# Windowed attention and two feed-forward stages on one core: PSUM shared out in halves of banks during the attention

## The chip, the cores and the metric

The kernel runs on one core of one Trainium2 chip. The metric is the device time of one execution in microseconds (us); the time of a kernel is the median of several runs. The core has a matrix engine (TensorE, PE in the profile, its weight loads PEld), a vector engine (VectorE, DVE), an activation engine (ScalarE, ACT), GpSimd (POOL) and queues for DMA (SP). Matrix products land in PSUM, which has eight banks; one bank holds 512 fp32 numbers for each of 128 partitions. DVE and ACT read the products from there.

## The reference

```python
# q, k, v: (4, 8, 576, 64), causal attention in a window of 64
scores = scale * q @ k.T ;  mask = (rel >= 0) & (rel < 64)
x = softmax(where(mask, scores, -1e9)) @ v        # -> (2304, 512)
# feed-forward 1: d_model 512, d_ff 1536
xn = x / sqrt(mean(x*x) + 1e-6) * rms_g
x = (silu(xn @ w_gate) * (xn @ w_val)) @ w_out
# feed-forward 2: d_model 512, d_ff 2048
out = (relu(x @ w_in) ** 2) @ w_out2
```

## The kernel before

All is kept transposed (features on the partitions). Each matrix product of the feed-forward parts is made of three: both operands are split into a high and a low part, and high times high, low times high and high times low are added up in PSUM (lines L608, L610, L612).

**Attention.** There are 36 blocks of 64 tokens. For a block PE makes the scores (L430), DVE adds the mask (L435), ACT takes the exponential (L437), PE transposes (L443), ACT or DVE copies (`pt`), PE multiplies by v (L453), DVE scales into `acc` (L458), and ACT or DVE sums the squares (L463, L465). Four blocks make a tile of 256 tokens, nine tiles in all. For a tile `rms` makes one small product (L479) and about nine tiny DVE instructions for the normalising factor, and then for each of the four blocks: DVE writes the normalised block into one of two buffers `xw` (L502), PE transposes it in two pieces (L506), ACT or DVE copies the high part from PSUM (L510, recorded by the helper at L238), and DVE subtracts for the low part (L511, recorded at L239).

**Feed-forward 1, first stage.** While the attention of later tiles goes on, the first two of the twelve slices of d_ff are worked on for each tile of 256 tokens: `up` makes for each slice two products of 12 matmuls (gate and value), ACT takes tanh of the gate (L653), two DVE instructions combine them (L654 reads the gate, L655 the value), and ACT and DVE split the result (`ah`, `al`). `down` makes four products of 6 matmuls, and ACT or DVE copies them to `acc`. So the first stage has 9 x 4 products of 12 matmuls and 8 x 4 of 6 ahead of the second stage. The second stage, on tiles of up to 512 tokens, begins at 171 us of the span, and feed-forward 2 comes behind it.

**PSUM.** Each `ps[i]` is one bank. Scores use banks 4 and 5, the transposes of the softmax 6, the products with v 7. The feed-forward products take whole banks 0, 1, 2 in turn (`mm_ring`), though a product of 256 columns fills half of one. `rms` uses bank 3 (`R_BANK`): the small product is in its first half, and the four blocks of a tile take its two halves in turn (`half`).

**Order.** Nothing is issued in the order in which the program is written. `Schedule.add` records a step with the keys that it reads and writes and a cost; `issue` then runs through a model of the engines and emits the steps in the order in which they could start there. Its keys for `rms` are those of the halves, `("ps", 3, 0)` and `("ps", 3, 1)`, and for the products those of whole banks. The semaphores are not set from these keys: the framework below sets them from the emitted order and the memory that instructions touch. Until the first product, PE's idle time in that model is filled with products nobody reads (L1015, into bank 0).

Of the kernel before, what the change touches and what calls it, by code (L numbers as in the profile page):

```python
# [16 lines left out]
ALU = mybir.AluOpType  # L17
# [13 lines left out]
EPS = 1e-6  # L31
# [196 lines left out]
def attn_moe_moe2(ctx: ExitStack, tc: tile.TileContext, qT, kT, vw, w1, w2, w3, w4, rms_g, out):  # L228
# [76 lines left out]
        return [("R", off // G32 + i) for i in g]  # L305

    ps = [psum.tile([P, 512], F32, name=f"ps{i}") for i in range(8)]
    mm_ring = Ring([0, 1, 2])

    fp = first_ctx.enter_context(tc.tile_pool(name="first", bufs=1, side="right"))  # L310
    s_ring = ring(fp, "s", S1, [P, N1])
# [21 lines left out]
    def at(*a, **k):  # L333
        attn_steps.append(sc.add(*a, **k))
# [134 lines left out]
        return ("pe", 0.45, 0.28, scores, [q] + kk, sk, 0.0), ("", softmax), ("pe", 0.46, 0.24, pv, [v, pt], [xk], 0.02), ("", result)  # L469


    half = [0]

    def rms(t, rank, part):
        nb = t[1]
        r = small["r"].next()
        ss = ps[R_BANK][:, :nb]
        m, y, z = (T[r][:, i, :nb] for i in range(3))
        at("pe", 0.3, lambda: nc.tensor.matmul(ss, T["comb"], T[part][:, :nb], start=True, stop=True), r=[(part, i) for i in range(nb)] + ["comb"], w=[("ps", R_BANK, 0)], rank=rank)  # L479
        tiny = lambda fn, rd=(): at("dve", 0.07, fn, r=rd, w=[r])  # L480
        tiny(lambda: nc.vector.tensor_scalar(m, ss, 1.0 / DM, EPS, op0=ALU.mult, op1=ALU.add), [("ps", R_BANK, 0)])


        tiny(lambda: nc.vector.tensor_scalar(y.bitcast(I32), m.bitcast(I32), -0.5, float(0x5F3759DF), op0=ALU.mult, op1=ALU.add))
        tt = lambda o, i, j: tiny(lambda: nc.vector.tensor_tensor(o, i, j, op=ALU.mult))
        stt = lambda o, i, j, v, op: tiny(lambda: nc.vector.scalar_tensor_tensor(o, i, v, j, op0=op, op1=ALU.mult))
        tt(z, m, y)
        tt(z, z, y)
        stt(z, z, z, -10.0 / 3.0, ALU.add)
        stt(y, z, y, 5.0, ALU.add)  # L490
        tt(z, m, y)
        stt(z, z, y, -0.5 * RS * RS, ALU.mult)
        stt(y, z, y, 1.5, ALU.add)
        for i, n in enumerate(blks(t)):
            half[0] ^= 1
            xw = xw_ring.next()
            pk = ("ps", R_BANK, half[0])
            x = T["acc"][:, :, n * WIN : (n + 1) * WIN]
            hi, lo = (xview(c, n * WIN, WIN) for c in ("xh", "xl"))
            x_ps = ps[R_BANK].rearrange("p (e i k) -> p e i k", e=2, i=2)[:, half[0]]  # L500
            kk = lambda c, n=n: allk(c, (n, 1))
            at("dve", c_dve(256), lambda i=i, x=x, xw=xw: nc.vector.scalar_tensor_tensor(T[xw].rearrange("p (a d) -> p a d", a=NP), x, T[r][:, 1, i : i + 1], T["gg"], op0=ALU.mult, op1=ALU.mult), r=[r, "gg"] + kk("acc"), w=[xw], port=True)  # L502

            def turn(xw=xw, x_ps=x_ps):
                for j in range(2):
                    nc.tensor.transpose(x_ps[:, j], T[xw][:, j * P : (j + 1) * P], T["ident"])  # L506

            at("pe", 0.108 * 2 + 0.1, turn, r=[xw, "ident"], w=[pk], rank=rank + 0.01 * (i + 1))
            xt = x_ps.rearrange("p i (h s) -> p (i h) s", h=2)
            at(AD, c_ad(256, True), lambda e, xt=xt, hi=hi: copy(e, hi, xt), r=[pk], w=kk("xh"))  # L510
            at("dve", c_dve(256), lambda xt=xt, hi=hi, lo=lo: sub(lo, xt, hi.bitcast(F32)), r=[pk] + kk("xh"), w=kk("xl"))  # L511
# [509 lines left out]
    def record(k):  # L1021

        stage, fs, t = seq[k]
        ends = [f for f in fs if end_of[stage, f] == k]
        if k < n_first:
            at_until(T1[min(k + 1, n_first - 1)])
            if k == n_first - 1:
                closed.append(sc.add("none", 0.001, close, after=list(attn_steps)))
                free.extend(range(W0, W0 + W1))
        if k == n_first:  # L1030
            flush()
            closed2.append(sc.add("none", 0.001, close2, after=list(first_steps) + closed))
            mm_ring.extend([3, 4])
            EXTRA[:] = 0.09, 0.1, 0.25
            a_ring.slots, a_ring.i = list(range(A1, A1 + A2)), 0
            s_ring.slots, s_ring.i = [f"s{S1 + i}" for i in range(S2)], 0
        if k >= n_first:
            while jobs and len(jobs) > n_jobs * (1 - (k - n_first + 1) / (len(seq) - n_first)):
                fn, *more = jobs.pop(0)
                fn(*more)  # L1040
        prefetch()
        a = {}
        for pos, f in enumerate(fs):
            a[f] = up(stage, f, t)
            if f in ends:
                for m in range(2):
                    free.append(w_slot.pop((stage, f, m)))
                prefetch()
            if pos == min(state.get("hold", 0), len(fs)) - 1:
                flush()  # L1050

        def finish():
            down(stage, fs, a, t, first_of[stage, t[0]] == k)
            for f in ends:
                free.append(w_slot.pop((stage, f, "down")))
            prefetch()


        state["prev"], state["hold"] = finish, min(2, len(a_ring.slots) - len(fs))
# [120 lines left out]
```

## Time and profile before

| | us |
|---|---|
| median of 3 runs | 914.86 (913.35 to 915.72) |
| profiled execution, its own time | 914.39 |
| its span, first to last instruction | 912.7 |
| PE busy | 894.8 (98% of the span) |
| PEld / DVE / ACT busy | 839.3 / 698.0 / 573.1 |

The time of the profiled execution is 1.7 us above its span and 0.5 us below the median. Busy time counts an engine's instructions; that of PE is modelled, since matmuls overlap. The granted TensorE clock is full from the first slice to the last. A row of waits names the instruction that waited, the one that released it, the sum, the count and the longest.

### The profile page before, as it was taken

The page shows a single profiled execution, that of the slowest core. Times are in us where ns is not written, and L with a number is a line of the kernel's source. Part 1 is how long each engine was busy: PE and PEld are TensorE (multiplying, and loading weights), DVE is VectorE, ACT ScalarE, POOL GpSimd, SP SyncE. Part 2 cuts the span into 40 slices and gives each one's busy share as a digit, 9 for nine tenths or more (in the row PEclk, how much of TensorE's full clock was granted, in tenths as well). Part 3 has the DMA queues.
Part 4 walks back from the last instruction along what each step waited for, and adds up shares of the span by engine and source line. Part 5 has one row for each costly group of instructions (what it writes and reads, how often), then busy time and mean ns, then how long its engine had stood idle before and what let it go on. Part 6 is the DMA issues. An engine that isn't in the chain of part 4 may idle for free.

```text
span 912.7 us, 17324 instructions
## 1 busy us (share of the span) xinstructions
PE 894.8 (98%) x6598; PEld 839.3 (92%) x6598; DVE 698.0 (76%) x1663; ACT 573.1 (63%) x1227; POOL 42.7 (5%) x45
## 2 busy tenths in 40 slices
PE   7889999999999999999999999999999999999997
PEld 6778899989988988988988999999999999999997
DVE  5999987677767877777768558667789976777786
ACT  6998875666666667666667556655557655555561
POOL 1000000000000100000000000000002300000011
PEclk9999999999999999999999999999999999999999
DMA  8856520246535735534556136272717373718142
GB/s 248 267 180 216 164 87 2 93 163 240 181 109 179 239 124 179 204 113 169 189 199 231 56 115 211 79 249 75 267 57 270 106 269 107 274 51 288 36 169 98
DMA packets 67203, 149.50 MB, mean 164 GB/s; under 512 B 6704, under 2 KB 25136, under 8 KB 67120
## 3 DMA queue, kind: packets, MB, share of 16 engines
q1 hardware_dynamic: 66592, 148.26, 47.6%
q8 instruction: 52, 0.85, 0.4%
q14 instruction: 31, 0.25, 0.1%
q10 hardware_dynamic: 528, 0.13, 0.1%
HBM read 114.30 MB, written 34.08 MB: 163 GB/s over the span
## 4 chain that ended last, share of the span: by engine, by line
PE 86%; DVE 11%; DMA 1%; ACT 1%; issue 1%
PE ps L884 19%; PE ps L820 18%; PE ps L608 15%; PE ps L610 15%; PE ps L612 15%; DVE sm L435 2%; DVE R L239 1%; DVE Q L239 1%; DVE xw L502 1%; PE ps L453 1%; DVE acc L458 1%; PE ps L430 1%; PE ps L443 1%; PE ps L1015 1%; DMA Q<-w 1%
## 5 line engine op out<-in xcount | busy, mean ns | idle before, releaser
L820 PE MATMUL ps<-R 128*128 128x288 f32 x1344 | 187.5, 296 | 0.8 <-DVE ps L238 0.6
L820 PEld LDWEIGHTS ps<-R 128*128 128x128 f32 x1344 | 181.6, 189 | 1.8 <-DVE ps L238 0.8
L884 PE MATMUL ps<-L,R 128*128 128x288 f32 x630 | 169.7, 297 | 1.5 <-DVE acc L892 1.3
L884 PE MATMUL ps<-Q,L 128*128 128x288 f32 x480 | 133.4, 297 | 0.0
L884 PEld LDWEIGHTS ps<-L,R 128*128 128x128 f32 x630 | 118.6, 188 | 2.5 <-DVE acc L892 2.0
L608 PE MATMUL ps<-R 128*128 128x256 f32 (+3 forms) x444 | 99.8, 347 | 0.6 <-ACT R L238 0.6
L610 PE MATMUL ps<-R 128*128 128x256 f32 (+3 forms) x444 | 97.6, 342 | 0.0
L612 PE MATMUL ps<-R 128*128 128x256 f32 (+3 forms) x444 | 97.3, 341 | 0.0
L238 ACT CAST L<-Q 128x512 fp32r<-128x512 f32 (+3 forms) x104 | 57.3, 565 | 62.7 <-DVE Q L651 56.0
L892 DVE TENSOR_TENSOR acc<-ps,acc 128x288 f32<-128x288 f32 x136 | 61.5, 456 | 41.0 <-PE ps L884 38.5
L884 PEld LDWEIGHTS ps<-Q,L 128*128 128x128 f32 x480 | 90.7, 189 | 0.0
L608 PEld LDWEIGHTS ps<-R 128*128 128x128 f32 x444 | 75.1, 189 | 8.0 <-ACT R L238 0.7
L610 PEld LDWEIGHTS ps<-R 128*128 128x128 f32 x444 | 75.6, 189 | 6.6
L612 PEld LDWEIGHTS ps<-R 128*128 128x128 f32 x444 | 75.6, 189 | 6.6
L238 DVE COPY acc<-ps 128x448 f32<-128x448 f32 (+4 forms) x81 | 47.8, 590 | 38.6 <-PE ps L612 19.4
L651 DVE TENSOR_TENSOR Q<-ps,Q 128x512 f32<-128x512 f32 (+2 forms) x50 | 31.9, 638 | 59.1 <-PE ps L612 57.4
L238 ACT COPY acc<-ps 128x288 f32<-128x288 f32 (+4 forms) x108 | 47.3, 439 | 42.0 <-PE ps L884 27.4
L240 DVE TENSOR_TENSOR L<-Q,L 128x512 fp32r<-128x512 f32 (+2 forms) x94 | 71.0, 761 | 1.9 <-ACT L L238 1.8
L868 ACT CAST L<-Q 128x576 fp32r<-128x576 f32 (+1 forms) x45 | 33.9, 756 | 59.1 <-PE ps L884 59.0
L681 ACT COPY ps<-acc 128x448 f32<-128x448 f32 (+2 forms) x97 | 53.1, 554 | 23.3 <-DVE acc L238 21.4
L239 DVE TENSOR_TENSOR Q<-Q 128x288 f32<-128x288 f32 (+1 forms) x96 | 60.0, 625 | 3.5 <-ACT Q L833 0.4
L437 ACT ACTIVATE sm<-sm,nb 128x128 f32<-128x128 f32 (+1 forms) x144 | 55.4, 388 | 10.4 <-DVE nb L435 10.4
(124 smaller groups left out, 1722.4 us busy)
## 6 DMA issues: line engine op xcount, KB each, us to landing
Q<-w SPq DMA_DIRECT2D x68, 512.0 KB, 4.4
R<-su SPq DMA_DIRECT2D x16, 1024.0 KB, 6.1
su<-L SPq DMA_DIRECT2D x24, 512.0 KB, 3.2
sd<-L SPq DMA_DIRECT2D x24, 512.0 KB, 3.2
R<-su SPq DMA_DIRECT2D x16, 768.0 KB, 5.0
v<-vw SPq DMA_DIRECT2D x36, 256.0 KB, 3.8
R<-sd SPq DMA_DIRECT2D x8, 1024.0 KB, 5.7
L<-sd SPq DMA_DIRECT2D x8, 1024.0 KB, 7.7
```

The lines of the kernel that those rows point to most:

```text
L238: copy = lambda e, out, in_: nc.scalar.copy(out, in_) if e == "act" else nc.vector.tensor_copy(out, in_)
L239: sub = lambda out, a, b: nc.vector.tensor_tensor(out, a, b, op=ALU.subtract)
L240: two = lambda e, out, a, b, op: (nc.vector if e == "dve" else nc.gpsimd).tensor_tensor(out, a, b, op=op)
L437: at("act", 0.39, lambda p=p: nc.scalar.activation(T[sm][:, p, :nk], T[sm][:, p, :nk], AF.Exp, bias=T[nb][:, p : p + 1], scale=-1.0, accum ...
L608: nc.tensor.matmul(acc, wh, xh, start=(i == 0 and not seeded), stop=False, skip_group_check=seeded)
L610: nc.tensor.matmul(acc, wl, xh, start=False, stop=False, skip_group_check=seeded)
L612: nc.tensor.matmul(acc, wh, xl, start=False, stop=(i == n - 1), skip_group_check=seeded)
L681: add("act", c_act(n), lambda b=b, dst=dst: nc.scalar.copy(ps[b][:, :n], dst), r=keys("acc", c, t), w=[("ps", b)])
L820: nc.tensor.matmul(bank, w_, x_, start=(start and i == 0), stop=(i == len(terms) - 1), skip_group_check=True)
L868: sc.add("act", c_act(m * PN), lambda z=z, o=o, m=m: nc.scalar.copy(z("h"), e(o, m)), r=ek(o, m), w=bk("h"))
L884: nc.tensor.matmul(bank, w_, x_, start=(start and i == 0), stop=(i == len(terms) - 1), skip_group_check=True)
L892: sc.add("dve", c_dve(PN), lambda: nc.vector.tensor_tensor(y(i, j), src, y(i, j), op=ALU.add), r=[key], w=yk(i, j))
```

## The change

Banks 0 and 1 are each cut in two halves of 256 columns, and during the first stage the feed-forward products take these four halves in turn: 0 first half, 0 second half, 1 first half, 1 second half. Bank 2 is thereby free and goes to `rms`, whose small product and whose blocks take four halves in turn, of banks 3, 2, 3, 2. With the second stage the products go back to whole banks, as before five of them, in the order 2, 3, 4, 0, 1 (before 3, 4, and then 0 to 2 from where the ring stood). The keys of the schedule are now those of the halves.

```diff
     ps = [psum.tile([P, 512], F32, name=f"ps{i}") for i in range(8)]
-    mm_ring = Ring([0, 1, 2])
+    for b in range(2):
+        ps += [ps[b][:, N1 * h : N1 * (h + 1)] for h in range(2)]
+        sc.names["ps", b] = [("ps", 8 + 2 * b + h) for h in range(2)]
+    mm_ring = Ring([8, 9, 10, 11])
...
-    half = [0]
+    r_ring = Ring([(3, 0), (2, 0), (3, 1), (2, 1)])
+    r_part = lambda r: ps[r[0]][:, N1 * r[1] : N1 * (r[1] + 1)]
...
-        ss = ps[R_BANK][:, :nb]
+        rs = r_ring.next()
+        ss = r_part(rs)[:, :nb]
...
-        tiny(lambda: nc.vector.tensor_scalar(m, ss, 1.0 / DM, EPS, op0=ALU.mult, op1=ALU.add), [("ps", R_BANK, 0)])
+        tiny(lambda: nc.vector.tensor_scalar(m, ss, 1.0 / DM, EPS, op0=ALU.mult, op1=ALU.add), [("ps", *rs)])
...
-            half[0] ^= 1
+            rt = r_ring.next()
             xw = xw_ring.next()
-            pk = ("ps", R_BANK, half[0])
+            pk = ("ps", *rt)
...
-            x_ps = ps[R_BANK].rearrange("p (e i k) -> p e i k", e=2, i=2)[:, half[0]]
+            x_ps = r_part(rt).rearrange("p (i k) -> p i k", i=2)
...
-            mm_ring.extend([3, 4])
+            mm_ring.slots, mm_ring.i = [2, 3, 4, 0, 1], 0
```

The change moves no work to another engine by itself, but the order that the model emits is another one. Lines of the changed kernel stand five further on: L506 is L511, L608, L610 and L612 are L613, L615 and L617, L653, L654 and L655 are L658, L659 and L660. In the rows below ps_64 is bank 0, ps_65 bank 1, ps_66 bank 2 and ps_67 bank 3, and what stands in brackets is the engine whose semaphore the instruction waits for (Activation is ACT).

The first place is on PE: the transposes of the four blocks of the first tile, before the change.

```order
L506 MATMUL ps_67<-ident,xw_109 128x128 [waits DVE_49]
L506 MATMUL ps_67<-ident,xw_109 128x128
L506 MATMUL ps_67<-ident,xw_110 128x128 [waits DVE_49]
L506 MATMUL ps_67<-ident,xw_110 128x128
L453 MATMUL ps_71<-v_100,pt_107 64x64 [waits DMAHW1_49]
L453 MATMUL ps_71<-v_100,pt_107 64x64 x7
L453 MATMUL ps_71<-v_101,pt_108 64x64 [waits DMAHW2_49,Activation_49]
L453 MATMUL ps_71<-v_101,pt_108 64x64 x7
L1015 MATMUL ps_64<-ident 128x128 x2
L506 MATMUL ps_67<-ident,xw_109 128x128 [waits DVE_49]
L506 MATMUL ps_67<-ident,xw_109 128x128
L506 MATMUL ps_67<-ident,xw_110 128x128 x2
```

And the same blocks with the change.

```order
L511 MATMUL ps_66<-ident,xw_109 128x128 [waits DVE_49]
L511 MATMUL ps_66<-ident,xw_109 128x128
L511 MATMUL ps_67<-ident,xw_110 128x128 [waits DVE_49]
L511 MATMUL ps_67<-ident,xw_110 128x128
L456 MATMUL ps_71<-v_100,pt_107 64x64 [waits DMAHW1_49]
L456 MATMUL ps_71<-v_100,pt_107 64x64 x7
L456 MATMUL ps_71<-v_101,pt_108 64x64 [waits DMAHW2_49,Activation_49]
L456 MATMUL ps_71<-v_101,pt_108 64x64 x7
L511 MATMUL ps_66<-ident,xw_109 128x128 [waits DVE_49]
L511 MATMUL ps_66<-ident,xw_109 128x128
L511 MATMUL ps_67<-ident,xw_110 128x128 [waits DVE_49]
L511 MATMUL ps_67<-ident,xw_110 128x128
```

The blocks now alternate between banks 2 and 3, and the two filler products ahead of the third block are gone.

The second place is on PE too: the two products of the second slice for the second tile, with the change; both are in bank 1, the first in its first half, the second in its second.

```order
L484 MATMUL ps_67<-part_129,comb 128x4 [waits DVE_49,Activation_49]
L613 MATMUL ps_65<-R 128x256 x4
L615 MATMUL ps_65<-R 128x256 x4
L617 MATMUL ps_65<-R 128x256 x4
L446 MATMUL ps_70<-ident,sm_105 128x128 [waits Activation_49]
L446 MATMUL ps_70<-ident,sm_105 128x128 x2
L446 MATMUL ps_70<-ident,sm_105 128x128 [waits Activation_49]
L613 MATMUL ps_65<-R 128x256 [waits Activation_49]
L613 MATMUL ps_65<-R 128x256 x3
L615 MATMUL ps_65<-R 128x256 x4
L617 MATMUL ps_65<-R 128x256 x4
```

The second product begins with a wait for ACT; the ACT instruction that it waits for is the tanh (L658) that reads the first half of the same bank. Before the change the two products of a slice were in two banks.

The third place is on DVE: what it does with those two products. L659 reads the first half of bank 1, L660 the second, with the change.

```order
L491 SCALAR_TENSOR_TENSOR r_130<-r_130 128x4 [waits DVE_49]
L659 SCALAR_TENSOR_TENSOR s_76<-s_76,ps_65 128x256 [waits PE_49,Activation_49]
L491 SCALAR_TENSOR_TENSOR r_130<-r_130 128x4 [waits DVE_49]
L239 TENSOR_TENSOR al_82<-s_75,ah_81 128x256 [waits Activation_49]
L507 SCALAR_TENSOR_TENSOR xw_109<-acc,r_130,gg 128x256 [waits DVE_49]
L507 SCALAR_TENSOR_TENSOR xw_110<-acc,r_130,gg 128x256
L660 SCALAR_TENSOR_TENSOR s_76<-s_76,ps_65 128x256
```

Before the change, the same step for the second slice stood thus (bank 0 holds the gate, bank 1 the value).

```order
L654 SCALAR_TENSOR_TENSOR s_76<-s_76,ps_64 128x256 [waits Activation_49]
L485 TENSOR_TENSOR r_130<-r_130 128x4 [waits DVE_49]
L435 ISA sm_106,nb_113<-ps_69,mask 128x128 [waits PE_49]
L435 ISA nb_113 128x1
L486 SCALAR_TENSOR_TENSOR r_130<-r_130 128x4 [waits DVE_49]
```

L659 has a wait for PE that L654 had not: the PE instruction is the last matmul of the second product, in the other half of the bank. The work queued behind it on DVE, the normalising of the next blocks (L491, L507), comes after it in DVE's order.

## Rows read from the trace of the kernel before

**Rows 1.** Busy time by stretch: PE, PEld, DVE, ACT, POOL, clock, DMA.

```profile
core 0: us, PE busy (x) PEld busy (x) DVE busy (x) ACT busy (x) POOL busy (x), PEclk, DMA share, GB/s
0.00:20.00 20.00, 14.90 (x204) 12.31 (x206) 10.09 (x53) 11.30 (x39) 3.08 (x15) 1.00 0.81 251
20.00:120.00 100.00, 92.96 (x1325) 83.30 (x1324) 97.85 (x504) 86.98 (x317) 0.00 (x0) 1.00 0.64 201
120.00:171.00 51.00, 51.00 (x562) 49.44 (x561) 39.74 (x158) 33.83 (x107) 0.00 (x0) 1.00 0.15 50
171.00:912.00 741.00, 735.96 (x4515) 694.29 (x4513) 550.35 (x953) 440.98 (x767) 39.66 (x30) 1.00 0.47 164
```

**Rows 2.** Who PE waited for from 20 to 171 us: sum, times, longest.

```profile
PE ps L506 <- DVE R L239: 3.9, 6, 0.8
PE ps L506 <- DVE xw L502: 1.2, 2, 0.8
PE ps L608 <- ACT R L238: 0.6, 1, 0.6
PE ps L479 <- DVE part L465: 0.5, 1, 0.5
PE ps L453 <- DVE acc L458: 0.4, 1, 0.4
PE ps L443 <- ACT pt L238: 0.4, 1, 0.4
PE ps L430 <- DVE nb L435: 0.3, 1, 0.3
```

**Rows 3.** Timeline around the third block of a tile (start, length, engine, line).

```profile
65.06 0.76 DVE L239 TENSOR_TENSOR R<-ps,R 128x256 fp32r<-128x256 f32 x2
...
65.87 0.44 PE L506 MATMUL ps<-ident,xw 128*128 128x128 f32 x2 [0.78 <-DVE R L239]
```

**Rows 4.** Who DVE waited for from 20 to 120 us.

```profile
DVE s L655 <- PE ps L612: 0.8, 1, 0.8
DVE R L239 <- ACT R L238: 0.3, 1, 0.3
DVE Q L557 <- DMA Q<-w: 0.2, 1, 0.2
DVE acc L458 <- PE ps L453: 0.2, 1, 0.2
```

**Rows 5.** Timeline of one product of 12 matmuls and its first readers.

```profile
147.03 0.64 PE L608 MATMUL ps<-R 128*128 128x256 f32 x4
...
147.51 0.64 PE L610 MATMUL ps<-R 128*128 128x256 f32 x4
...
147.99 0.64 PE L612 MATMUL ps<-R 128*128 128x256 f32 x4
...
148.47 0.28 PE L479 MATMUL ps<-part,comb 128*128 128x4 f32 x2
...
148.73 0.38 ACT L653 ACTIVATE s<-ps 128x256 f32<-128x256 f32 x1 [0.64 <-PE ps L612]
```

**Rows 6.** Groups by line and shape, 20 to 171 us: busy, mean ns, idle before.

```profile
L506 PE MATMUL ps<-ident,xw 128*128 128x128 f32 x72 | 12.6, 284 | 5.1 <-DVE R L239 3.9 <-DVE xw L502 1.2
L655 DVE SCALAR_TENSOR_TENSOR s<-s,ps 128x256 f32<-128x256 f32 x18 | 7.5, 418 | 2.5 <-PE ps L612 2.3
L654 DVE SCALAR_TENSOR_TENSOR s<-s,ps 128x256 f32<-128x256 f32 x18 | 7.5, 416 | 3.1 <-ACT s L653 3.1
L653 ACT ACTIVATE s<-ps 128x256 f32<-128x256 f32 x18 | 6.8, 379 | 6.1 <-PE ps L612 6.1
```

More of the change, by code (lines that the diff above doesn't have):

```diff
@@ L476, in rms @@
         r = small["r"].next()
-        ss = ps[R_BANK][:, :nb]
+        rs = r_ring.next()
+        ss = r_part(rs)[:, :nb]
         m, y, z = (T[r][:, i, :nb] for i in range(3))
-        at("pe", 0.3, lambda: nc.tensor.matmul(ss, T["comb"], T[part][:, :nb], start=True, stop=True), r=[(part, i) for i in range(nb)] + ["comb"], w=[("ps", R_BANK, 0)], rank=rank)
+        at("pe", 0.3, lambda: nc.tensor.matmul(ss, T["comb"], T[part][:, :nb], start=True, stop=True), r=[(part, i) for i in range(nb)] + ["comb"], w=[("ps", *rs)], rank=rank)
         tiny = lambda fn, rd=(): at("dve", 0.07, fn, r=rd, w=[r])
-        tiny(lambda: nc.vector.tensor_scalar(m, ss, 1.0 / DM, EPS, op0=ALU.mult, op1=ALU.add), [("ps", R_BANK, 0)])
+        tiny(lambda: nc.vector.tensor_scalar(m, ss, 1.0 / DM, EPS, op0=ALU.mult, op1=ALU.add), [("ps", *rs)])
         tiny(lambda: nc.vector.tensor_scalar(y.bitcast(I32), m.bitcast(I32), -0.5, float(0x5F3759DF), op0=ALU.mult, op1=ALU.add))
```

## The prediction, before the changed kernel was run

> **What bounds the kernel now.** I read the busy time by stretch first [rows 1]. Only the first stage, up to 171 us, is touched: behind it the products stand in five whole banks as before, under other numbers. PE works 894.83 of 912 us, so the time is PE's work plus what PE stands idle, and the idle time is 5.1 us up to 20 us, 7.04 from 20 to 120, none from 120 to 171 and 5.04 behind. The reader should see two things in [rows 1]. From 20 to 120 us DVE is the fullest engine (97.85 of 100), ACT has 86.98, PE 92.96: three engines that feed each other in a ring, with little air. From 120 us on PE has a backlog and never stops, so every microsecond that PE loses earlier is paid in full at the end, and so is one lost from 120 to 171.
>
> Next the waits of PE [rows 2]. The largest is the one that the change goes for: the transposes L506 wait for DVE's L239, 3.9 us in 6 waits, 0.65 each. L239 is the subtraction that reads a transposed block out of bank 3. The feed-forward products (L608) never wait for a bank: their one wait, 0.6, is for their operand. So three whole banks are enough for the products, and one bank is not enough for `rms`. The most that the change can give is the 3.9 of that row, or 5.1 with the waits for `xw`, but these hang on DVE writing `xw` and on two buffers, which stay.
>
> Then what sort of wait that is [rows 3]. Blocks take the two halves of bank 3 in turn, so the third block goes where the first was. Its transposes start at 65.87, and the two subtractions (of the first and of the second block) run from 65.06 to 65.82. The third block therefore waited for the reader of the other half too. The schedule's keys know halves; the built program keeps engines apart by bank.
>
> **The change, part by part.** *Transposes.* Four blocks of a tile in banks 3, 2, 3, 2: the third needs only the first block's readers. I counted, in the emitted orders of the first stage, the instructions of PE that wait for a reader of a bank standing at most 11 instructions ahead in the program (all engines counted; such a reader has hardly begun when PE arrives). Before there are 11 among the transposes and 2 among the products, 13 in all. With the change there are 7 among the transposes. So a part of the wait stays, since the model, believing four halves free, lets third blocks come early.
>
> *Products.* Here is the price. The two products of a slice are now in one bank, and so are the pairs of `down`. Where the reader of the first is emitted ahead of the second, PE cannot begin the second until that reader is done; the second order piece of the change shows such a place, with the tanh (L658) between. Counted in the same way there are 16 such products with the change, against 2. What one costs, no row shows for products; the nearest rows are the transposes. A product of 12 matmuls starts every 1.44 us, and its first reader begins 0.26 us after the product could be followed (148.47 to 148.73) and takes 0.38 [rows 5]; so 0.64 is lost where nothing stands between, and nothing where 0.6 us of other matmuls do. From the transposes: 3.9 us for 13 places is 0.30 each with those that cost nothing counted, and 0.65 where a wait is seen at all. I take 0.30, since between the halves there often stand four softmax transposes or 16 products of the scores. 7 + 16 = 23 places at 0.30 are 6.9 us; 3.9 us go; net +3.0 us. The ends: 23 at 0.65 are 15.0, net +11; all at nothing is -3.9.
>
> *DVE.* Where the second product is emitted ahead of the reader of the first, the reader waits for the whole second product. That holds up DVE or ACT, and behind it the softmax and the normalising of later blocks (the third order piece: L507 stands behind L659). Up to 120 us I count 4 such places close together on DVE. Each costs between nothing and one product, 1.44 us [rows 5]; the one wait of DVE for a product that the trace has in that stretch is 0.8 [rows 4]. 4 at 0.8 are 3.2 us on the fullest engine. Half of it, 1.6, I count as reaching PE, since PE has work of its own in the meantime; the ends are 0 and 5.8. Behind 120 us ACT and DVE wait more often, but the groups of L653, L654 and L655 wait 6.1, 3.1 and 2.5 us there already [rows 6] without PE losing anything, so I count that at nothing; the cover is 11 us of free DVE and 17 of free ACT [rows 1], and if it fails the wait shows in the first item.
>
> *What moves besides.* The choice between ACT and DVE in the emitted order shifts: DVE gets fewer casts of transposed blocks and fewer squares, and more copies of `pt` and `acc`. In instructions of about equal length this comes out even, so I count nothing. The filler products L1015 fill time that is idle anyway. A stall of PE lets DVE catch up, and some of the other 3.1 us of waits from 20 to 120 (7.04 less 3.9) then vanish: I take 1.0 off, between 0 and 3.1.
>
> **The sum.** 3.0 + 1.6 - 1.0 = +3.6 us on the profiled execution's 914.39, which is 918.0. The median of the runs shown is 0.47 above that execution, so 918.5 us is forecast for the median, 0.4% above 914.86.
>
> The halves are where a rule decides. The third block's start in [rows 3] is that of a bank kept whole. The Trainium skill, "PSUM — Partial Sum Buffer", section "PSUM bank collisions raise a hardware error", says that accesses of two engines have to be kept apart by bank and quadrant and not by address, because different columns of one bank collide as well. By that rule four halves in two banks give products and readers no more freedom than two banks do; by the schedule's keys they would be four separate places. The trace agrees with the rule, in the 0.05 us between the end of the second subtraction and the start.
>
> **The rivals.** *Faster: the halves serve.* If the near places cost the products nothing, as the 2 among the products before the change did (L608 has no bank wait in [rows 2]), and the third blocks find their bank free, the 3.9 us go and nothing comes: 914.86 - 3.9 = 911.0. For it: a product's reader can be covered by 0.6 us of other matmuls, and often is. Against it: 16 places are many, and in some the reader sits in a queue of DVE, which has no air. It decides if a place costs below 0.17 us on the mean (3.9 / 23). Chance 0.18.
>
> *The same: one wait for another.* From 20 to 120 us DVE sets the pace and its work is not changed. PE then stands idle for what DVE leaves, about 7 us, wherever the stall is written down; the new waits take the place of the old. Time 914 to 917. For it: 97.85 of 100 us on DVE. Against it: PE's lost time is paid behind 120 us, where DVE has air, and some of the 16 places lie behind 120 us. Chance 0.27.
>
> *Worse: DVE is held up.* The four places on DVE cost a whole product each and PE loses 0.65 at each of its places: +11 + 5.8 at the extreme; with half of the excess over the forecast, 925. For it: DVE has nothing to win the time back with. Against it: DVE lags behind PE in this stretch, so that the second product is often done when DVE comes to it. Chance 0.10.
>
> *Forecast*, 916 to 922: chance 0.45.
>
> **How the numbers follow.** About 0.3% (2.7 us: 912.1 to 917.6) is what a measurement of this kernel can tell from no change. Faster by more: the faster rival but for its upper edge, 0.17. Within: the second rival, the lower edge of the forecast and the upper one of the first, 0.33. Slower: 0.50. The range goes from the faster rival, 911, to 925; the forecast's own range is 916 to 922.
>
> **What would show it.** Right: the row of transposes waiting for L239 is smaller than 3.9 but not gone; new rows have L613 waiting for DVE or ACT readers (L238, L658, L659, L660), 4 to 7 us in sum; DVE has new waits of L659 for L617 ahead of 120 us; PE's idle time up to 171 us grows from 12 by about 4; the second stage begins some 4 us later; behind it the stretch is as long as before. Wrong: no row of L613 waiting for readers (then the halves serve), or PE's idle time from 20 to 120 still near 7 with other names (then DVE was the bound). A difference behind 171 us would be a thing that I have not seen: I count it at nothing because the order there is that of five whole banks again, but the ring starts at another bank.

## The result, and the profile of the changed kernel

The changed kernel takes 922.82 us (median of 4 runs, 922.23 to 923.95) against 914.59 in the runs beside it: ratio 1.0091, 95% interval 1.0077 to 1.0105. It is 8.2 us slower. One kernel further on, e1, had two of its five executions disturbed (1090 and 1937 us), the profiled one among them; its time and ratio below are those of the other three, and its trace is not read. The profiled execution of the changed kernel took 922.23 us with a span of 920.5. The stretches of [rows 1], of the changed kernel, in the same columns:

```profile
core 0: us, PE busy (x) PEld busy (x) DVE busy (x) ACT busy (x) POOL busy (x), PEclk, DMA share, GB/s
0.00:20.00 20.00, 14.99 (x220) 12.62 (x221) 11.08 (x61) 12.36 (x42) 3.08 (x15) 1.00 0.85 267
20.00:120.00 100.00, 90.78 (x1264) 80.39 (x1264) 94.28 (x471) 86.33 (x321) 0.00 (x0) 1.00 0.64 197
120.00:171.00 51.00, 47.67 (x540) 43.93 (x540) 36.28 (x159) 29.34 (x101) 0.00 (x0) 1.00 0.10 30
171.00:912.00 741.00, 738.59 (x4542) 696.67 (x4541) 553.65 (x958) 445.31 (x776) 39.84 (x30) 1.00 0.47 165
```

PE stands idle 9.22 us from 20 to 120 (7.04 before) and 3.33 from 120 to 171, where it had not been idle at all. DVE has become emptier (94.28 against 97.85), and the clock is full throughout. The second stage begins with the first matmul of 512 columns. The timelines give it as 171.14 us in the kernel before and 179.00 in the changed one:

```profile
171.14 1.08 PE L608 MATMUL ps<-R 128*128 128x512 f32 x4
```

```profile
179.00 1.08 PE L613 MATMUL ps<-R 128*128 128x512 f32 x4
```

From there to the end both take 741.5 us (912.7 less 171.14, 920.5 less 179.00). The whole loss, 7.9 us, lies in the first stage. Comparing the starts of its products one by one, the changed kernel is level at 92.2 us, 2.3 late when the kernel before is at 122.2, 6.1 late at 138.7 and 7.3 at 156.7: 5.5 us of the loss, some two thirds, come behind 122 us.

Who PE waited for, from 20 to 179 us, answering to [rows 2]:

```profile
PE ps L613 <- ACT s L658: 1.7, 3, 0.8
PE ps L613 <- ACT acc L238: 1.5, 2, 1.2
PE ps L433 <- DVE nb L438: 1.4, 2, 1.1
PE ps L511 <- DVE xw L507: 1.4, 2, 0.8
PE ps L446 <- ACT R L238: 1.2, 1, 1.2
PE ps L511 <- DVE R L238: 1.0, 2, 0.7
PE ps L511 <- DVE R L239: 0.9, 1, 0.9
PE ps L613 <- ACT R L238: 0.7, 1, 0.7
PE ps L484 <- DVE nb L438: 0.6, 1, 0.6
PE ps L613 <- DVE s L660: 0.5, 1, 0.5
PE ps L446 <- ACT s L658: 0.5, 1, 0.5
PE ps L613 <- DVE s L659: 0.4, 1, 0.4
```

The transposes' wait for readers of their bank fell from 3.9 to 1.9 (L511 for L239 and for L238 on DVE). The products, which had no bank wait, now have 4.1 us of them (1.7, 1.5, 0.5 and 0.4). Together that is 2.1 us more. PE's other waits, among them those of the softmax steps (L433, L446), grew from 3.4 to 5.8. All rows together make 4.5 of the 7.9 us, and 2.1 of these 4.5 are waiting for banks; the loss must be looked for elsewhere as well. The readers' groups show more, up to 179 us, answering to [rows 6]:

```profile
L659 DVE SCALAR_TENSOR_TENSOR s<-s,ps 128x256 f32<-128x256 f32 x18 | 7.5, 419 | 14.1 <-ACT s L658 7.7 <-PE ps L617 5.5 <-ACT sm L440 0.8
L660 DVE SCALAR_TENSOR_TENSOR s<-s,ps 128x256 f32<-128x256 f32 x18 | 7.5, 416 | 0.5 <-PE ps L617 0.4
...
L658 ACT ACTIVATE s<-ps 128x256 f32<-128x256 f32 x18 | 6.8, 378 | 10.2 <-PE ps L617 10.2
```

L658 (the tanh) and L659 read the gate, the first product of a pair. They waited 6.1 and 3.1 us before and now 10.2 and 14.1; L660, which reads the value, went from 2.5 to 0.5. The readers of the first half are late, those of the second are not. Ahead of 120 us DVE's waits, answering to [rows 4], are:

```profile
DVE s L659 <- PE ps L617: 2.3, 2, 1.4
DVE s L659 <- ACT sm L440: 0.8, 1, 0.8
DVE acc L238 <- PE ps L617: 0.7, 1, 0.7
```

One pair shows the mechanism, in the timeline of the changed kernel at 132 us (start, length, engine, line, and in brackets the idle time before it and what ended it), answering to [rows 5]:

```profile
133.55 0.64 PE L617 MATMUL ps<-R 128*128 128x256 f32 x4
...
134.03 0.64 PE L613 MATMUL ps<-R 128*128 128x256 f32 x4
...
134.99 0.64 PE L617 MATMUL ps<-R 128*128 128x256 f32 x4
...
135.67 0.38 ACT L658 ACTIVATE s<-ps 128x256 f32<-128x256 f32 x1 [1.52 <-PE ps L617]
...
136.09 0.42 DVE L659 SCALAR_TENSOR_TENSOR s<-s,ps 128x256 f32<-128x256 f32 x1 [1.48 <-ACT s L658]
```

The gate's last matmuls end at 134.19, and PE goes straight on with the value, in the other half of the bank, from 134.03 to 135.63. The tanh starts at 135.67: ACT stood idle 1.52 us, about one product (1.44), for numbers that were finished, and DVE stood idle 1.48 behind it. In [rows 5], with whole banks, the reader came 0.26 us after the end of its product's slot. Four microseconds later the same program shows the other form, the one that the prediction priced:

```profile
139.74 0.41 DVE L659 SCALAR_TENSOR_TENSOR s<-s,ps 128x256 f32<-128x256 f32 x1
...
140.21 0.74 PE L613 MATMUL ps<-R 128*128 128x256 f32 x4 [0.36 <-DVE s L659]
```

Here the gate's reader is emitted ahead of the value, and the value waits for it, 0.36 us.

Waits do not add up to the whole. To the beginning of the second stage PE is idle 17.6 us against 12.1, which is 5.4 more; its busy time is 161.43 against 159.01 with about as many instructions (2085 and 2086). Added up over the trace, the time from the start of the matmul ahead of a product to the product's own first matmul is 7.2 us for the 68 products before and 14.8 after: 7.6 us lie at the beginnings of products, and L613's idle time there is only 5.3 against 0.6 for L608:

```profile
L613 PE MATMUL ps<-R 128*128 128x256 f32 x144 | 25.0, 296 | 3.0 <-ACT s L658 1.7 <-ACT R L238 0.7 <-DVE s L659 0.4
...
L613 PE MATMUL ps<-ah,R 128*128 128x256 f32 x64 | 14.4, 306 | 2.3 <-ACT acc L238 1.5 <-DVE s L660 0.5
```

Up to 0.16 us of a wait behind another product does not show as idle, since the last four matmuls of a product are drawn 0.64 long while the next four could start after 0.48 [rows 5].

### The profile page after: what moved, and what is told of

The parts are those of the page before. It is cut to its first block, busy times and chain, and to the rows that moved or that the text cites. A ratio compares the mean times of both kernels' runs of the same rounds, so it can differ in the third digit from the quotient of the medians.

```text
span 920.5 us, 17333 instructions
## 1 busy us (share of the span) xinstructions
PE 897.2 (97%) x6596; PEld 838.6 (91%) x6596; DVE 698.6 (76%) x1654; ACT 573.3 (62%) x1236; POOL 42.9 (5%) x45
## 4 chain that ended last, share of the span: by engine, by line
PE 87%; DVE 11%; issue 1%; ACT 1%; DMA 0%; DVEq 0%; ACTq 0%
PE ps L889 18%; PE ps L825 18%; PE ps L613 16%; PE ps L615 15%; PE ps L617 15%; DVE sm L438 1%; PE ps L456 1%; DVE R L239 1%; PE ps L433 1%; DVE xw L507 1%; DVE Q L239 1%; PE ps L446 1%; DVE acc L461 1%; PE ps L1020 1%; PE ps L511 0%
## 5 line engine op out<-in xcount | busy, mean ns | idle before, releaser
L613 PE MATMUL ps<-R 128*128 128x256 f32 (+3 forms) x444 | 99.4, 346 | 3.0 <-ACT s L658 1.7
L615 PE MATMUL ps<-R 128*128 128x256 f32 (+3 forms) x444 | 97.5, 341 | 0.0
L617 PE MATMUL ps<-R 128*128 128x256 f32 (+3 forms) x444 | 97.2, 341 | 0.0
L238 ACT CAST L<-Q 128x512 fp32r<-128x512 f32 (+3 forms) x104 | 57.3, 566 | 62.5 <-DVE Q L656 55.1
L613 PEld LDWEIGHTS ps<-R 128*128 128x128 f32 x444 | 75.0, 188 | 11.7 <-ACT s L658 3.0
L615 PEld LDWEIGHTS ps<-R 128*128 128x128 f32 x444 | 75.5, 189 | 6.7
L617 PEld LDWEIGHTS ps<-R 128*128 128x128 f32 x444 | 75.5, 189 | 6.6
L238 DVE COPY acc<-ps 128x448 f32<-128x448 f32 (+4 forms) x85 | 49.4, 582 | 39.5 <-PE ps L617 20.6
L238 ACT COPY acc<-ps 128x288 f32<-128x288 f32 (+4 forms) x104 | 45.7, 443 | 42.4 <-PE ps L889 27.4
L239 DVE TENSOR_TENSOR Q<-Q 128x288 f32<-128x288 f32 (+1 forms) x96 | 60.0, 625 | 3.5 <-ACT Q L838 0.4
```

The lines of the kernel that those rows point to most:

```text
L238: copy = lambda e, out, in_: nc.scalar.copy(out, in_) if e == "act" else nc.vector.tensor_copy(out, in_)
L239: sub = lambda out, a, b: nc.vector.tensor_tensor(out, a, b, op=ALU.subtract)
L613: nc.tensor.matmul(acc, wh, xh, start=(i == 0 and not seeded), stop=False, skip_group_check=seeded)
L615: nc.tensor.matmul(acc, wl, xh, start=False, stop=False, skip_group_check=seeded)
L617: nc.tensor.matmul(acc, wh, xl, start=False, stop=(i == n - 1), skip_group_check=seeded)
```

## The experiments

The prediction's theory was that PE is stopped in front of a product whose bank neighbour is still being read. The rival that the groups above suggest is that the readers of the first product, held until the second is done, are the greater cost. Ratios are to the kernel before, run beside each, with 95% intervals. Two figures counted from the emitted orders go with them: **held**, readers that wait for a product in the other half of their bank, and **near**, products that wait for a reader at most 11 instructions ahead (the prediction's count). The kernel before has 0 held and 2 near, the changed one 19 and 16.

**1. Two whole banks, with and without the other half of the change.** In the first the changed kernel's products take two whole banks; in the second the same is done to the kernel before, so the normalising keeps one bank; the third gives the kernel before the four halves alone.

```diff
# e1: the changed kernel
-    mm_ring = Ring([8, 9, 10, 11])
+    mm_ring = Ring([0, 1])
# e10: the kernel before
-    mm_ring = Ring([0, 1, 2])
+    mm_ring = Ring([0, 1])
...
# e2: the kernel before
-    mm_ring = Ring([0, 1, 2])
+    for b in range(2):
+        ps += [ps[b][:, N1 * h : N1 * (h + 1)] for h in range(2)]
+        sc.names["ps", b] = [("ps", 8 + 2 * b + h) for h in range(2)]
+    mm_ring = Ring([8, 9, 10, 11])
...
```

With the second stage e10, e2 and the kernels built like them below go back to the five whole banks; those lines are left out here.

> The four halves for the transposed blocks stay; the feed-forward products take two whole banks (0 and 1) in turn instead of four halves of them, so no product shares a bank with a reader of another product. Theory (PE is stopped by the reader of the other half of a bank): in the emitted order 9 products still wait for a reader close ahead of them, 16 with the change; at 0.5 us each the time is some 3.5 us below the changed kernel, 918 to 920. Rival (two banks instead of three are too few, however they are cut): as slow as the changed kernel, 922, or slower, since two whole banks hold two products and four halves hold four.

> The kernel before with two whole banks for the products in the first stage instead of three, and the normalising as before in bank 3; bank 2 stands empty. It gives the price of the third bank, and beside the run with two whole banks and the new normalising the worth of the second bank for the normalising. Theory: 12 products wait for a reader close ahead, 10 transposes; the third bank is worth 4 to 6 us, so 918 to 921, and the second bank for the normalising up to 2 us. Rival (the second bank for the normalising is worth nothing or does harm): 917 to 918.8, not above the run with the new normalising.

> The products take four halves of banks 0 and 1 as in the change; the normalising is as before, in the two halves of bank 3 alone; bank 2 stands empty in the first stage. Theory: 10 products wait for a reader close ahead (16 with the change) and 11 transposes (7 with the change, 11 before), so about +5 us on the kernel before: 919 to 921. Rival (the second bank for the normalising is what does harm, by the other order that it makes): within 2 us of the kernel before, 913 to 916.5.

Measured: e1 918.17 us, 1.0051 (1.0035 to 1.0067); e10 920.03, 1.0068 (1.0053 to 1.0083); e2 923.95, 1.0114 (1.0099 to 1.0129). With the normalising in two banks the halves cost 0.40% more than the plain two banks that they are made of (1.0091 against 1.0051), with it in one bank 0.46% (1.0114 against 1.0068). Four halves are not as good as two banks but worse. The second bank for the normalising seems to be worth 0.2% (1.0114 to 1.0091, 1.0068 to 1.0051), some 2 us, though in each of the two pairs the intervals overlap. e2 is dearer than its 10 near products made it (919 to 921 us expected).

**2. The schedule told the truth.** In e5 the changed kernel's keys are those of banks; in e4 the two products of a bank are recorded as one step, so that the model knows that their readers come after both.

```diff
# e5
-        sc.names["ps", b] = [("ps", 8 + 2 * b + h) for h in range(2)]
+        for h in range(2):
+            sc.names["ps", 8 + 2 * b + h] = [("ps", b)]
# e4, in up; down likewise, two products at a time
-            pe(12 * c_mm(n), mm, r=xk + [f"wh{k}", f"wl{k}"], w=[("ps", b)])
...
+            two_mm.append((mm, xk + [f"wh{k}", f"wl{k}"], ("ps", b)))
...
+            pe(24 * c_mm(n), lambda: [x[0]() for x in two_mm], r=sum((x[1] for x in two_mm), []), w=[x[2] for x in two_mm])
```

> As the change, with the same four halves in memory, but the schedule's keys for the products are those of the banks, so the model knows that a product waits for the readers of the other half. Theory (the loss comes from an order that the model would not emit if it knew of the banks): 9 products wait for a reader close ahead, 16 with the change, 9 in the kernel with two whole banks; so like that one, 918 to 920. Rival (sharing a bank costs by itself, in whatever order): 922 or more.

> As the change, but the two products that share a bank are recorded as one step of the schedule (24 matmuls, or 12), so that no reader and no other product of PE can come between them. Theory (PE loses at readers that stand between the two): one product is left that waits for a reader close ahead, so most of the 8.2 us come back: 914 to 917. Rival (the readers that wait for the second product, on ACT and DVE, are what costs): such waits rise from 19 to 31 places, so slower than the changed kernel, 923 to 927.

Measured: e5 919.02, 1.0050 (1.0033 to 1.0067); e4 917.21, 1.0032 (1.0018 to 1.0046), second stage at 172.26. With the same banks an order made from what the banks allow wins back nearly half (e5) to two thirds (e4). e4 speaks for the prediction's theory and against the rival: 31 readers are held, more than in the changed kernel, for which the rival expected 923 to 927 us, and one product is near, for which the theory expected 914 to 917. PE's products there wait for no bank; their one row, from 20 to 172 us, is for an operand:

```profile
PE ps L613 <- ACT R L238: 0.8, 2, 0.5
```

A count of held readers is thus no price either. That they cost less where the order reckons with them is a reading, not shown, since e4 changes the order along with the counts.

**3. The same order, other partners.** In e7 the halves are taken as bank 0, bank 1, bank 0, bank 1. The instructions of every engine come in the same order as in the changed kernel; only the places differ. Consecutive products now lie in different banks: 3 readers are held instead of 19, but 24 products are near instead of 16.

```diff
-    mm_ring = Ring([8, 9, 10, 11])
+    mm_ring = Ring([8, 10, 9, 11])
```

> The changed kernel with its instructions in exactly the same order on every engine; only the places differ: consecutive products go to different banks (0, 1, 0, 1), so a product shares its bank with the one two before it. Products that wait for a reader close ahead rise from 16 to 24; readers on ACT and DVE that wait for a product in the other half fall from 19 to 3. Theory (PE stopped by readers of the other half): slower than the changed kernel by some 4 us, 925 to 929. Rival (readers delayed by the second product): faster by 3 us or more, below 920. Rival (the order alone is what costs): as the changed kernel, 922 to 924.

Measured: 917.10, 1.0042 (1.0027 to 1.0057), some 4.5 us less than the changed kernel (0.49% by the two ratios). Its rows, in the columns of [rows 1], and the waits of ACT and DVE from 20 to 174 us:

```profile
20.00:120.00 100.00, 90.47 (x1279) 80.68 (x1281) 94.33 (x473) 86.71 (x320) 0.00 (x0) 1.00 0.64 197
120.00:171.00 51.00, 50.43 (x574) 48.37 (x563) 40.09 (x163) 31.92 (x106) 0.00 (x0) 1.00 0.15 51
```

```profile
ACT s L658 <- PE ps L617: 7.0, 8, 1.2
...
DVE s L659 <- ACT s L658: 4.5, 3, 2.8
DVE s L659 <- PE ps L617: 3.3, 2, 2.3
```

The rival's expectation came true, and the theory's, 925 to 929 us, did not: with half as many near places again the kernel is faster. Its products do wait for readers, but at 24 near places for 3.0 us in all, where the changed kernel has 4.1 at 16:

```profile
PE ps L613 <- ACT s L658: 2.2, 2, 1.1
...
PE ps L613 <- DVE s L660: 0.8, 1, 0.8
```

What else got better is the tanh (10.2 to 7.0), L659 behind it (7.7 to 4.5) and PE from 120 to 171 us (3.33 us idle to 0.57), while PE's idle time from 20 to 120 is much the same (9.53 against 9.22). Since both kernels issue the same, their matmuls can be compared one by one: of the 5.1 us by which e7's second stage begins earlier (173.95 against 179.00), 3.9 lie at the beginnings of products and 0.8 at the softmax transposes. PE still pays at the products, and less than before: the readers that it waits for are themselves held less often. That this is why is a reading of these rows.

**4. Is it the order?** e15 gives the kernel before a slightly different emitted order by one constant of its model.

```diff
-LEAD = 20.0
+LEAD = 21.0
```

> The kernel before with nothing changed but one number of the schedule: the attention is given a lead of 21 us instead of 20, so that the order in the first stage differs a little and all memory is the same. It shows what an order that was not chosen by trying costs. Theory: within 2 us of the kernel before, 912.5 to 916. Rival (the kernel before sits at an order found by trial, and any other costs 3 us or more): 917 to 922.

Measured: 915.44, 1.0021 (1.0011 to 1.0032). This one other order costs 0.2%, not 0.9%. It does not bound what another order may cost: e12 below shares no bank and takes 1.1% more. Only the kernels that keep an order and move the places (3, 5 and 6) tell the two apart.

**5. The order of the kernel before, only the places changed.** e16 issues exactly what the kernel before issues; its three places are the halves of bank 0 and the first half of bank 1. e17 adds the second bank for the normalising at the same order.

```diff
# e16: the kernel before
-    mm_ring = Ring([0, 1, 2])
+    ps += [ps[0][:, :N1], ps[0][:, N1:], ps[1][:, :N1]]
+    sc.names["ps", 0], sc.names["ps", 1] = [("ps", 8), ("ps", 9)], [("ps", 10)]
+    mm_ring = Ring([8, 9, 10])
...
# e17: e16 and this
-        ss = ps[R_BANK][:, :nb]
+        ss = ps[3][:, :nb]
...
-            x_ps = ps[R_BANK].rearrange("p (e i k) -> p e i k", e=2, i=2)[:, half[0]]
+            x_ps = ps[3 - half[0]].rearrange("p (e i k) -> p e i k", e=2, i=2)[:, half[0]]
```

> The kernel before with its instructions in exactly the same order on every engine; only the places of the three product slots differ: bank 0 first half, bank 0 second half, bank 1. It is the price of two products sharing a bank with no change of order: 12 products wait for a reader close ahead (2 before) and 15 readers for a product in the other half. Theory (sharing costs): 12 at 0.46 us, 5 us and more with what the readers lose: 919 to 923. Rival (the order is what costs): within 1.5 us of the kernel before, 913 to 915.6.

> As the run with the same order and three halves, and also the two halves for the transposed blocks are put into two banks (3 and 2), again with the instructions of the kernel before in their order. Beside that run it is the worth of the second bank for the normalising: the 3.9 us that transposes wait for the reader of the other half. Theory: 1 to 3 us faster than that run. Rival (DVE sets the pace, so the wait only goes elsewhere): within 1 us of it.

Measured: e16 922.75, 1.0102 (1.0085 to 1.0119); e17 919.74, 1.0067 (1.0052 to 1.0082). Two products in one bank, at an unchanged order, are enough to lose 9.3 us. 15 readers are held and 12 products near, so the two are not told apart here. In e16 the waits of PE, and then of ACT and DVE, from 20 to 179 us are

```profile
PE ps L610 <- DVE s L657: 4.3, 5, 1.5
PE ps L508 <- DVE R L239: 4.3, 5, 1.3
```

```profile
ACT s L655 <- PE ps L614: 6.6, 4, 3.4
ACT acc L238 <- PE ps L614: 5.6, 5, 2.6
...
DVE s L656 <- ACT s L655: 4.7, 4, 1.5
DVE s L657 <- PE ps L614: 3.9, 3, 1.8
DVE s L656 <- PE ps L614: 3.8, 2, 2.6
```

Both forms are there: the tanh (L655 in this kernel) waits up to 3.4 us, and PE up to 1.5 for L657. Matmul by matmul, 6.6 of the 8.0 us by which the second stage begins later (179.10 against 171.14) lie at the beginnings of products. In e17 the transposes' wait is down to

```profile
PE ps L508 <- DVE R L239: 1.0, 4, 0.3
```

3.3 us of wait less, and 3.0 us less time: that part of the change does what the diff says.

**6. Six halves: sharers next to each other, and three apart.** e3 gives the kernel before six halves of banks 0 to 2, so consecutive products share a bank; 20 readers are held and 6 products near. e21 takes the same order of instructions and the same halves, but first all first halves, then all second ones: 0 held, 3 near.

```diff
# e3: the kernel before
+    for b in range(3):
+        ps += [ps[b][:, N1 * h : N1 * (h + 1)] for h in range(2)]
+        sc.names["ps", b] = [("ps", 8 + 2 * b + h) for h in range(2)]
-    mm_ring = Ring([0, 1, 2])
+    mm_ring = Ring(range(8, 14))
...
# e21: e3 and this
-    mm_ring = Ring(range(8, 14))
+    mm_ring = Ring([8, 10, 12, 9, 11, 13])
```

> The products take six halves of banks 0, 1 and 2; the normalising is as before. The number of banks is that of the kernel before, only that two products share one. Theory: 6 products wait for a reader close ahead (2 before), at 0.5 to 0.65 us each some +2 to +3 us on the kernel before: 916 to 918. Rival (the number of banks decides): as before, 913.5 to 915.5.

> The kernel with six halves of banks 0 to 2 for the products, in the same instruction order, but the halves are taken in the order first halves of banks 0, 1, 2, then their second halves, so that consecutive products stand in different banks and each shares a bank with the product three before it. With consecutive products in one bank this order took 920.0 us, ratio 1.0072. Theory A (the cost is that the readers of a product are held until the next one, in the other half of its bank, is finished): gone here, since three products later the readers are long done; 913.5 to 916 us, ratio 0.999 to 1.002. Theory B (sharing a bank costs, however the sharers are placed): 919 to 921 us, ratio 1.006 to 1.008.

Measured: e3 920.02, 1.0072 (1.0057 to 1.0087); e21 913.23, 0.9992 (0.9983 to 1.0001). The 0.8% are gone with one line that moves no instruction. e3 is dearer than its near products made it (916 to 918 us expected), and the three that go with e21 cannot be worth 7 us at the 0.46 to 0.65 us that were reckoned for one. Matmul by matmul, of the 7.4 us between the two second stages 2.8 lie at the transposes of the normalising, 2.3 at the beginnings of products and 1.4 at the softmax transposes: most of it lies at steps that touch no bank of products, which fits readers that hold up what stands behind them on DVE and ACT. The gate's combining L657 in e3 (up to 177 us) and in e21 (up to 170):

```profile
L657 DVE SCALAR_TENSOR_TENSOR s<-s,ps 128x256 f32<-128x256 f32 x18 | 7.5, 416 | 12.6 <-PE ps L615 7.2 <-ACT s L656 4.1 <-PE ps L482 1.3
```

```profile
L657 DVE SCALAR_TENSOR_TENSOR s<-s,ps 128x256 f32<-128x256 f32 x18 | 7.4, 414 | 3.1 <-ACT s L656 3.1
```

12.6 us of waiting against 3.1, which is what the kernel before has [rows 6]. The Trainium skill, "Perfetto Trace Analysis", section "Optimizing Tensor Performance", asks that independent groups of matmuls rotate through different PSUM banks so that ACT and DVE read one out while the next is made. These two kernels agree with it: the same six halves cost 0.8% where they follow each other in one bank, and nothing measurable where they rotate.

**7. Pairs as one step elsewhere.** e11 does to e3 what e4 does to the changed kernel; e12 does it to the kernel before, as a control.

> Six halves of three banks for the products, the normalising as before, and the two products of a bank in one step, so that no reader stands between them. Theory (the reader between the two is what costs in the six halves, 5.9 us): within 1.5 us of the same pairs in whole banks, which run beside it. Rival (readers that wait for the second product cost): 3 us or more above those pairs in whole banks, since 31 readers wait for the other half here and none there.

> The kernel before, with three whole banks, but the products of a pair in one step of the schedule: it shows what the pairing does by itself. If the pairing is neutral: 913 to 916. If longer steps of PE hold up the softmax: 917 to 919, and then the gain of the pairs in the changed kernel was larger than it looked.

Measured: e11 920.84, 1.0072 (1.0057 to 1.0087); e12 923.91, 1.0109 (1.0094 to 1.0124). Against e3 nothing is won, although its near products go from 6 to 3 while its held readers go from 20 to 31. Both expectations of e11 missed: it is neither within 1.5 us of e12 nor 3 above it, but 3 below. The control was badly chosen: a pair that needs two of three banks always needs one of the pair before. So the gain of e4 is not a rule, and why e11 gains nothing is open. What e12 does show is that an order alone, with no bank shared, can cost 1.1%.

**8. Can the normalising have its second bank for nothing?** e18 is the kernel before, in its own order, with the second place of the blocks moved to bank 2, beside one product place. e22 takes five halves for the products, rotating, and the sixth for the normalising, in the model's own order.

```diff
# e18: the kernel before
-            x_ps = ps[R_BANK].rearrange("p (e i k) -> p e i k", e=2, i=2)[:, half[0]]
+            x_ps = ps[2 if half[0] else 3].rearrange("p (e i k) -> p e i k", e=2, i=2)[:, half[0]]
# e22: the changed kernel
-    mm_ring = Ring([8, 9, 10, 11])
+    ps += [ps[2][:, :N1]]
+    sc.names["ps", 2] = [("ps", 12), ("ps", 2, 1)]
+    mm_ring = Ring([8, 10, 12, 9, 11])
...
-    r_ring = Ring([(3, 0), (2, 0), (3, 1), (2, 1)])
+    r_ring = Ring([(3, 0), (2, 1), (3, 1), (2, 1)])
```

> The kernel before, in its own instruction order, with products in three whole banks as before; only the second of the two places of the transposed normalised blocks moves from bank 3 to bank 2, where it stands beside one of the three product places. Theory A (the second bank for the normalising is worth some 3 us, and sharing hurts where two consecutive products or a product and its neighbour's reader follow each other closely): the wait of the transposes for L239 falls from 3.9 to about 1, and the loss in bank 2 is smaller than that; 911 to 914 us, ratio 0.997 to 1.000. Theory B (any sharing with a product place costs more than the wait that it removes): 916 to 920 us, ratio 1.002 to 1.006, with new waits of the products for L239 or of the transposes for the readers L653 to L655.

> Products in five halves, taken as first halves of banks 0, 1, 2, then second halves of 0 and 1, so that no two consecutive products share a bank; the second half of bank 2 goes to the normalising, whose small product and blocks take bank 3 first half, bank 2 second half, bank 3 second half, bank 2 second half in turn. The order is the model's own for these places. Theory A (consecutive sharers are the whole cost; a second bank for the normalising is worth some 2 to 3 us, and beside one product place it costs about 2 again): 911 to 915 us, ratio 0.997 to 1.001, second stage at 169 to 172 us. Theory B (each bank that products and normalising share costs by itself, and the order adds to it): 916 to 920 us, ratio 1.002 to 1.007, with products waiting for L239 by more than 2 us.

Measured: e18 914.62, 1.0006 (0.9997 to 1.0015); e22 919.48, 1.0053 (1.0039 to 1.0066). In e18 the waits of PE from 20 to 171 us are

```profile
PE ps L506 <- DVE R L239: 1.6, 2, 1.3
PE ps L608 <- DVE R L239: 1.3, 2, 1.1
...
PE ps L506 <- ACT s L653: 0.3, 1, 0.3
```

2.3 us leave the transposes, and 1.3 of them stand with the products, as new waits for the same subtractions. It lies between what the two theories expected: the wait is passed on rather than removed. e22 has the time that theory B expected without its waits (no product waits for L239); its second stage begins at 176.46 with 4 held and 11 near, two of these for readers of transposes. The cause there was not found, and the rotation through the banks alone did not prevent it.

No version was measurably faster than the kernel before; e21 is level with it.

## Why the prediction was right in its sign and not in its size

**Right.** Forecast were 3.6 us more and 918.5 us in a range of its own of 916 to 922; measured were 8.2 more and 922.82. The way was right. The readers and products of one bank are kept apart as a whole bank, whatever the half: the tanh at 135.67 and the value at 140.21 show it for products, as [rows 3] did for transposes. The first stage alone is touched, and the stretch behind it is as long as before (741.5). The second bank helps the normalising, and part of its wait stays (3.9 to 1.9). New rows of products waiting for readers came to 4.1 us, at the lower edge of the 4 to 7 named. PE's idle time to 171 us went from 12.1 to 17.6, by 5.4 where "about 4" stood, and the second stage came 7.9 later where "some 4" stood. "The same: one wait for another" is out: DVE became emptier and PE still lost.

**The sum, in its own terms.** The item on transposes forecast 3.9 less 7 near places at 0.30, a gain of 1.8; the rows show 2.0. The 16 products at 0.30 forecast 4.8; the rows show 4.1. The item on readers forecast 1.6, and 1.0 was taken off because other waits should vanish, 0.6 in all; but PE's other waits grew by 2.4 (3.4 to 5.8), and another 3.4 us of the 7.9 are in no row of waits, 2.4 of them as a longer busy time. Even if all of these 3.4 belonged to near products, the items on readers and on vanishing waits together would be 2.4 and not 0.6. These rows book a wait where PE meets it, not where it arises.

**The step that failed** is the item on the readers, "Behind 120 us ACT and DVE wait more often ... so I count that at nothing; the cover is 11 us of free DVE and 17 of free ACT", and with it the 1.6 us for all held readers. The free time was there, and became more (DVE 36.28 busy in those 51 us against 39.74), but it was no cover: PE lost 3.3 us of idle time in that stretch, where it had lost none. What two products in a row in one bank cost was then measured at a fixed order: 0.8% (e3 to e21, with 20 held readers fewer and 3 near products fewer), and 0.5% between the changed kernel and e7, although e7 has 8 more near products. By e7 held readers were worth some 4.5 us (0.49%) or more, instead of 1.6, and by e3 some 7. Why the free time is no cover is argued and not shown: the held reader stands in the chain from product to tanh to combining to `ah` and `al` to `down`, and behind 120 us PE has ever less other work to put in between. No row has PE waiting for `ah` or `al`; what the rows name are the late readers themselves (L658, L659, L660) and the softmax steps that stand behind them.

**The price of a near place.** In the changed kernel 16 near products cost 4.1 us by the rows, 0.26 each, close to the 0.30 that was taken. That was in part luck, since it is no fixed price: e7 pays 3.0 us for 24, 0.13 each, e4 has one near product and 31 held readers and is 0.32% above the kernel before, and e18 and e21, with 8 and 3 near products, lost nothing measurable. Neither count gives the time by itself.

**Not counted at all** were the parts of waits at the beginnings of products that the drawn length of the matmuls hides, up to 0.16 us each. PE's busy time grew by 2.4 us over about the same instructions. That this is the hidden lateness is argued from the beginnings of products, which are 7.6 us later in all while their idle time grew by 4.7; it is not shown.

**Left open.** e7 is still 0.42% above the kernel before. An order planned for four free halves, 24 near products and 3 held readers are mixed there; an order alone cost 0.2% in e15 and 1.1% in e12. The rest is not divided further.

## What to carry to other kernels

In a program whose engines are kept apart by whole banks, as this one's are, a half of a PSUM bank is a place for data but not for overlap: of two products that follow each other in one bank, the second can hold up the first one's readers for its whole length (1.52 us in the pair shown). If banks must be halved, let the products rotate through the banks; that is one line and moves no instruction. Sharers three products apart cost nothing measurable in six halves (e21), sharers two apart were better than neighbours but not level with whole banks (e7), and e22, with sharers two and three apart and the normalising beside them, still lost 0.5%. Free time on the reading engines is not by itself a cover for a late reader: ask what waits behind it, above all in the stretch where the other work runs out.

## What the runs showed that was not expected

Four places in two banks were slower than the two banks as two places, by 0.40% and 0.46% in two settings: a schedule that believes in room that is not there did worse here than one with less room. And sharing a bank among products as such cost nothing measurable: six halves with sharers three products apart ran at 0.9992 of the kernel before, while two sharers in a row, at its very order, cost 9.3 us.
